# One DMA transpose in place of three pairs of PE transposes, and two moves on the DMA queue, in a block-sparse attention and spatial gating kernel

## The chip, the cores and the metric

The kernel runs on one core of a Trainium2 chip. The metric is the device time of one execution in microseconds (us), taken as the median over the timed runs. The engines are named as the profile names them: PE (TensorE, its matmuls), PEld (its weight loads), ACT (ScalarE), DVE (VectorE), POOL (GpSimd) and SP (SyncE, which issues nearly all DMAs here, in order).

## The reference

The input holds 4 batches with 8 heads, 768 positions and 64 dimensions a head. Block-sparse attention is followed by a gated feed-forward layer with a product along the sequence:

```python
scores = 1/sqrt(64) * q @ k^T                      # per batch and head, 768 x 768
scores[~mask] = -1e9                               # blocks of 32: window, edges, three sampled
attn = exp(scores - max) / sum                     # softmax
x = (attn @ v), heads side by side                 # (4, 768, 512)
h = relu(x @ w_in);  u, v = h[..., :512], h[..., 512:]
v_n = (v - mean(v)) / sqrt(var(v) + 1e-6)
v_s = w_spatial @ v_n + b_spatial                  # along the 768 positions
out = (u * v_s) @ w_out
```

## The kernel before

Heads are worked on in pairs, four pairs to a batch (pairs 0 to 3 are batch 0, 4 to 7 batch 1, and so on). A position list of 768 is six tiles of 128. For each pair, k and q are loaded, cast to bf16 (POOL), transposed so that the head's dimension lies on the partitions, and multiplied on PE; ACT takes the exponential out of PSUM into `a_all`; PE multiplies that with v (`ps_av`, one extra column gives the sum); DVE divides (`normalize`: `rc`, then `xn`). The result x is transposed once more into `xt`, so that PE can use it as the stationary operand against `w_in_t` in the feed-forward part, the class `Moe`.

The order of all instructions is written out by hand. A loop over slots `s` issues for each slot: the scores and the exponential of one unit (`qk_unit` in slots 0 to 35, `qk_full` from slot 36 on); the products with v that the table `AV_AT` puts into this slot; the functions registered with `when(slot, ...)`; `STEPS[slot]` matmuls from the queue of feed-forward steps (`run_queue`); and last the functions in `late[slot]`. Each engine works its instructions off in this order.

Batch 0 is worked in query thirds. `UNITS` lists the units: 0 and 1 are the heads of pair 0 for its first two thirds, 2 to 4 are pairs 1 to 3 in the first third, 5 to 7 pairs 1 to 3 in the second, and 8 to 11 pairs 0 to 3 in the last third, which is tiles 4 and 5 of the 768 positions. A unit takes three slots for its scores. Its normalized result is a small tile (`xn3`, two tiles of 128 by 128), and `xtr_third(u)` transposes it: two PE transposes against the identity into the spare columns of the unit's own `ps_av` bank (line 302), and one DVE copy of 128 by 256 into the pair's `xt` tile (line 221). It stands in `late` of slot 3u + 7, so slots 31, 34 and 37 for units 8, 9 and 10, and in slot 41 for unit 11. From pair 4 on, a whole pair's `xn` goes through one DMA transpose instead (`xtr_dma`, line 569).

The feed-forward products of tiles 4 and 5 of batch 0 ("v4 v5 u4 u5", four steps each, one for each pair in the order 0 to 3) are dealt into the queue in slot 42; the products with the spatial weights follow them, six steps to a tile.

Three things that the change touches go through SP. The spatial weights `w_spatial` come in six pieces (`ws_load`, line 578: four alone, the last two in one load), are cast by POOL two to a tile (`ws_cast`), and are transposed two at a time into `w_spt` by `ws_tr` (line 589) in slots 23, 27 and 31. The k, q and v of pair p are loaded by `load` (line 110; pair 6 in slot 31, pair 7 in slot 38), cast (pair 6 in slot 38), and k and q transposed by `tr_dma` into `tt` (line 444; pair 5 in slot 31, pair 6 in slot 40); `split` then copies `tt` into `kq` on DVE (line 221; pair 6 in slots 55 and 57). The load of `w_out` is registered in slot 44.

The scores lie in PSUM under the tag "sc" with two buffers of two banks each, the products with v under "av" with two buffers, and the feed-forward products in two single banks.

Of the kernel before, what the change touches and what calls it, by code (L numbers as in the profile page):

```python
# [10 lines left out]
FP32 = mybir.dt.float32  # L11
BF16 = mybir.dt.bfloat16
# [14 lines left out]
def kernel(  # L27
# [16 lines left out]
    nc = tc.nc  # L44

    B, H, S, D = q.shape
# [3 lines left out]
    NCH = S // 128  # L50
# [6 lines left out]
    NG = H // 2  # L57
# [5 lines left out]
    NT = 3  # L63
    TC = NCH // NT
# [6 lines left out]
    work = ctx.enter_context(tc.tile_pool(name="work", bufs=1))  # L71
# [379 lines left out]
    a_ref, av_ref, x_ref, xn_ref, xt_ref = {}, {}, {}, {}, {}  # L451


    UNITS = [("h", 0), ("h", 1)] + [(0, p) for p in range(1, NG)] + \
# [40 lines left out]
    def av_tile(key, n):  # L495
        ps = psum.tile([128, 512], FP32, tag="av", bufs=2, name="ps_av")
        av_ref[key] = ps[:, 0:n * VS].rearrange("p (c d) -> p c d", d=VS)
        x_ref[key] = ps[:, 512 - TW // 2:512].bitcast(BF16)

    def normalize(ps, out, n):  # L500
        rc = work.tile([128, NCH, 1], FP32, tag="rc", bufs=2)
        nc.vector.reciprocal(out=rc[:, 0:n], in_=ps[:, :, D:VA])  # L502
        nc.vector.tensor_tensor(out=out, in0=ps[:, :, 0:D],  # L503
                                in1=rc[:, 0:n].to_broadcast([128, n, D]), op=ALU.mult)

    def av_unit(u, e):
        t, p = UNITS[u]
        if e == 0:
            av_tile(u, 2 * TC)
        for i in range(8 * e, 8 * e + 8):  # L510
            g, ci = divmod(i, NCH)
            if t == "h":
                h, qc, to, n = p, g, g, 2 * TC
                pp = 0
            else:
                (h, qc), n, pp = divmod(g, TC), TC, p
                to = qc * 2 + h
            at = (h * NCH + ci) * n * 128 if t != "h" else ci * n * 128
            at += qc * 128
            nc.tensor.matmul(out=av_ref[u][:, to, 0:VA], lhsT=a_ref[u][:, at:at + 128],  # L520
                             rhs=vv[pp % NVV][:, h, ci, 0:VA],
                             start=(ci == 0), stop=(ci == NCH - 1))
        if e == 2:
            a_ref.pop(u)
            if t == "h":
                if p == 0:
                    xn_ref[0] = work.tile([128, 2 * TC, 2, D], BF16, tag="xn0", bufs=1, name="xn0")
                normalize(av_ref.pop(u), xn_ref[0][:, :, p, :], 2 * TC)
            else:
                xn_ref[u] = work.tile([128, TC, 2, D], BF16, tag="xn3", bufs=3, name="xn3")  # L530
                normalize(av_ref.pop(u), xn_ref[u].rearrange("p c h d -> p (c h) d"), 2 * TC)

    def av_full(j, qc):
# [14 lines left out]
    def xt_tile(p):  # L548
        if p not in xt_ref:
            xt_ref[p] = work.tile([128, S], BF16, tag="xt", bufs=7, name="xt")  # L550
        return xt_ref[p]

    def xtr_pe(p, xn, c0, n, ps=None):
        if ps is None:
            ps = bank()
        for c in range(n):
            tr(ps, c, pair_of(xn, c))
        dve_copy(xt_tile(p)[:, c0 * 128:(c0 + n) * 128], ps[:, 0:n * 128])

    def xtr_third(u):  # L560
# [4 lines left out]
        else:  # L565
            xtr_pe(p, xn_ref.pop(u), t * TC, TC, x_ref.pop(u))

    def xtr_dma(p):
        nc.sync.dma_start_transpose(
            out=xt_tile(p).rearrange("p (c n) -> p c n", c=NCH),  # L570
            in_=xn_ref.pop(("p", p)).rearrange("p c h d -> p (c h d)"))
# [2 lines left out]
    ws = {}  # L574

    def ws_load(i, n=1):
        t = work.tile([128, n, S], FP32, tag=f"ws_f{n}", bufs=4 if n == 1 else 1, name="ws_f")
        nc.sync.dma_start(out=t, in_=moe_w_spatial.rearrange("(p c) s -> p c s", c=NCH)[:, i:i + n])
        for k in range(n):
            ws["f", i + k] = t[:, k]  # L580
# [48 lines left out]
    class Moe:  # L629
# [9 lines left out]
            self.steps = 0  # L639

        def xt(self, g, tcc):
            return xt_ref[self.b * NG + g][:, tcc * 128:(tcc + 1) * 128]

        def v_product(self, tcc, grp):
# [121 lines left out]
    def when(slot, *fns):  # L766
        at.setdefault(slot, []).extend(fns)

    def c(f, *a, **kw):
        return lambda: f(*a, **kw)  # L770
# [14 lines left out]
    for p, sl in ((1, 12), (3, 18), (0, 21)):  # L785
        when(sl, c(tr_rest, p, 2 if p == 0 else 1))
    XT_AT = {1: 12, 3: 15, 5: 23, 11: 41}
    for u in range(1, len(UNITS)):
        late.setdefault(XT_AT.get(u, 3 * u + 7), []).append(c(xtr_third, u))
    late[15].append(c(tr_rest, 2))  # L790

    def moe_begin(b):
        moe[b] = Moe(b)
# [57 lines left out]
    def slot_of(p):  # L851
        return S0 + 12 * (p - NG)

    for p in range(NG, NP):
        g = slot_of(p)
        when({4: 13, 5: 22, 6: 31}.get(p, g - 34), c(load, p, "k"), c(load, p, "q"), c(load, p, "v"))
        when({4: 18, 5: 26, 6: 38}.get(p, g - 24),
             c(cast, p, "k", PL), c(cast, p, "q", PL), c(cast, p, "v", PL))
        when({4: 20, 5: 31}.get(p, g - (16 if p in (10, 14) else 20)), c(tr_dma, p))
        when(31 if p == 4 else g - (7 if p in (9, 13) else 5), c(split, p, 0))  # L860
        when(32 if p == 4 else g - 3, c(split, p, 1))
        if p == NP - 1:
            when(g + 20, last_x)
        else:
            when(g + (19 if p % NG == NG - 1 else 20), c(xtr_dma, p))
    for i, (ld, ca) in enumerate([(16, 19), (16, 21), (17, 23), (17, 25), (18, 27), (18, 29)]):
        if i < 5:
            when(ld, c(ws_load, i, 2 if i == 4 else 1))
        when(ca, c(ws_cast, i))
    for i, sl in enumerate((23, 27, 31)):  # L870
        when(sl, c(ws_tr, i))
    when(44, *[c(w_out_load, g) for g in range(NDH)])
    when(52, *[c(w_out_cast, g, PL) for g in range(NDH)])
# [8 lines left out]
    for s in range(NS + LAG + 2):  # L882
        if s < S0:
            qk_unit(*divmod(s, 3))
        elif s < NS:
            j, ci = divmod(s - S0, NCH)
            qk_full(j + H, ci)
        early = at.get(s, [])
        for u, e in av_at.get(s, []):
            av_unit(u, e)  # L890
        if 0 <= s - LAG - S0 and s - LAG < NS:
            j, qc = divmod(s - LAG - S0, NCH)
            av_full(j + H, qc)
        for f in early:
            f()
        run_queue(STEPS.get(s))
        for f in late.get(s, []):
            f()
        while post:
            post.pop(0)()  # L900
# [31 lines left out]
```

## Time and profile before

| | |
|---|---|
| median of 3 runs | 209.09 us (209.01 to 209.22) |
| profiled execution | 209.45 us, span 207.6 us |
| granted TensorE clock | 1.0 |
| PE busy | 202.7 us of the span |
| ACT busy | 167.0 us |
| DVE busy | 129.9 us |
| POOL busy | 75.4 us |
| DMA queue of SP | 40.78 MB, packets 76.8% of 16 engines' span |

The span runs from the first to the last instruction; the execution's own time has the launch around it. A row of a timeline gives start and length in us, the engine, the line of the kernel, the operation, what it writes and reads, and how many instructions were merged into it. PE's matmuls are pipelined, so that a busy PE may still have waited a little, and the distance between two starts says more than a duration. An SP row's length is the time of issuing; the landing of the data comes later.

### The profile page before, as it was taken

What the parts mean: (1) busy time and instruction counts of PE and PEld (TensorE: products, weight loads), DVE (VectorE), ACT (ScalarE), POOL (GpSimd) and SP (SyncE); (2) the same over time, 40 slices, a digit from 0 to 9 for tenths busy, and PEclk for the clock granted to TensorE, in tenths of its full rate; (3) what the DMA queues carried; (4) which work ended last, traced back from release to release, by engine and by line L of the source; (5) the groups of instructions that cost most, each with busy time, mean ns of one, the idle gap of its engine ahead of it and who ended that gap; (6) DMA issues with size and microseconds to landing.
All of it is one profiled execution on the core that took longest, in us unless ns stands there. A gap on an engine that the chain in (4) does not pass through costs nothing.

```text
span 207.6 us, 5255 instructions
## 1 busy us (share of the span) xinstructions
PE 202.7 (98%) x2128; PEld 127.2 (61%) x2128; DVE 129.9 (63%) x287; ACT 167.0 (80%) x222; POOL 75.4 (36%) x117
## 2 busy tenths in 40 slices
PE   8899999999999999999999999999999999999993
PEld 6689878766666666655655555655665556444441
DVE  7688697889654364648798355348685444567542
ACT  5899999999999999889999887998989883266022
POOL 6799899684680421310716402200202000003000
PEclk9999999999999999999999999999999999999999
DMA  5999999999999999999986549785101072810466
GB/s 141 345 364 347 345 406 297 234 278 303 230 356 193 264 272 171 319 318 262 299 91 182 162 88 279 179 246 125 38 3 38 0 92 51 285 72 0 50 152 255
DMA packets 65579, 42.21 MB, mean 203 GB/s; under 512 B 46740, under 2 KB 60436, under 8 KB 65556
## 3 DMA queue, kind: packets, MB, share of 16 engines
q1 hardware_dynamic: 64692, 40.78, 76.8%
q10 hardware_dynamic: 864, 1.11, 1.5%
q8 instruction: 16, 0.26, 0.5%
q14 instruction: 7, 0.06, 0.1%
HBM read 24.38 MB, written 6.29 MB: 148 GB/s over the span
## 4 chain that ended last, share of the span: by engine, by line
PE 93%; ACT 5%; issue 0%; DVE 0%; ACTq 0%
PE ps_moe L617 32%; PE ps L487 23%; PE ps_av L538 13%; PE ps_t L617 8%; PE ps L474 6%; PE ps_sc L617 5%; ACT a_all L479 5%; PE ps_av L520 4%; PE wps L182 1%; PE ps L302 1%; PE ps_av L302 1%; PE mq L309 0%; ACT osb L224 0%; PE psq L317 0%; PE ps L317 0%
## 5 line engine op out<-in xcount | busy, mean ns | idle before, releaser
L491 ACT ACTIVATE a_all<-ps 128x768 bf16<-128x768 f32 x144 | 112.8, 812 | 11.8 <-PE ps L487 5.3
L487 PE MATMUL ps<-kq 88*128 88x384 bf16 x288 | 70.4, 325 | 0.0
L538 PEld LDWEIGHTS <-a_all 128*128 128x128 bf16 x864 | 45.2, 97 | 20.0
L538 PE MATMUL ps_av<-vv,a_all 128*128 128x65 bf16 x864 | 49.8, 193 | 0.0
L487 PEld LDWEIGHTS <-kq 88*128 88x128 bf16 x288 | 27.7, 97 | 29.2 <-issue 0.3
L617 PE MATMUL ps_moe<-w_in_t,xt 128*128 128x512 bf16 x144 | 43.2, 378 | 0.0
L479 ACT ACTIVATE a_all<-ps 128x1024 bf16<-128x1024 f32 x36 | 34.1, 1026 | 2.5 <-PE ps L474 2.0
L617 PE MATMUL ps_moe<-vn,w_spt 128*128 128x512 bf16 x108 | 33.5, 378 | 0.0
L656 POOL TENSOR_SCALAR std<-mv 128x3 f32<-128x3 f32 (+1 forms) x9 | 2.9, 317 | 72.5 <-DVE mv L653 56.9
L138 POOL CAST nat<-st_k 128x768 bf16<-128x768 f32 (+2 forms) x18 | 14.6, 810 | 30.8 <-DMA st_k<-in_k_dram 29.9
L502 DVE RECIPROCAL rc<-ps_av 128x6 f32<-128x6 f32 (+1 forms) x36 | 6.7, 186 | 26.0 <-PE ps_av L538 23.2
L689 DVE SCALAR_TENSOR_TENSOR un<-ps_moe,b_col,un 128x512 bf16<-128x512 f32 x18 | 13.5, 749 | 14.8 <-PE ps_moe L617 14.8
L474 PE MATMUL ps<-kq 88*128 88x256 bf16 (+3 forms) x140 | 22.0, 279 | 0.7 <-ACT a_all L479 0.3
L617 PEld LDWEIGHTS <-xt 128*128 128x128 bf16 x192 | 15.4, 98 | 7.5 <-DVE xt L221 0.2
L503 DVE TENSOR_TENSOR xn<-ps_av,rc 128x384 bf16<-128x384 f32 (+1 forms) x36 | 18.5, 513 | 1.2
L617 PE MATMUL ps_moe<-w_out_t,gt 128*128 128x512 bf16 x60 | 17.6, 378 | 0.0
L652 DVE BATCH_NORM_STATS2 stats<-vn 128x6 f32<-128x512 bf16 x24 | 16.4, 683 | 1.3 <-ACT vn L647 0.9
L474 PEld LDWEIGHTS <-kq 88*128 88x128 bf16 (+1 forms) x140 | 12.8, 98 | 5.2 <-DVE kq L221 0.8
L138 POOL CAST nat<-st_q 128x768 bf16<-128x768 f32 (+2 forms) x21 | 14.8, 706 | 2.7 <-DMA st_q<-in_q_dram 2.2
L188 DVE TENSOR_SCALAR vn<-ps_moe 128x512 bf16<-128x512 f32 x18 | 12.3, 686 | 4.6 <-PE ps_moe L617 4.5
L617 PEld LDWEIGHTS <-w_spt 128*128 128x128 bf16 x144 | 11.7, 98 | 5.2
L221 DVE COPY kq<-tt 64x1536 bf16<-64x1536 bf16 x24 | 14.4, 598 | 0.4
(85 smaller groups left out, 208.7 us busy)
## 6 DMA issues: line engine op xcount, KB each, us to landing
st_v<-in_v_dram SPq DMA_DIRECT2D x16, 384.0 KB, 5.8
st_k<-in_k_dram SPq DMA_DIRECT2D x15, 384.0 KB, 4.7
out_dram<-osb SPq DMA_DIRECT2D x20, 256.0 KB, 2.8
st_q<-in_q_dram SPq DMA_DIRECT2D x12, 384.0 KB, 4.5
w_f<-in_moe_w_in_dram SPq DMA_DIRECT2D x6, 256.0 KB, 6.6
ws_f<-in_moe_w_spatial_dram SPq DMA_DIRECT2D x4, 384.0 KB, 7.2
w_f<-in_moe_w_out_dram SPq DMA_DIRECT2D x4, 256.0 KB, 4.2
st_q<-in_q_dram SPq DMA_DIRECT2D x6, 128.0 KB, 5.6
```

Of the source, the lines that this page charges most:

```text
L138: eng.tensor_copy(out=dst, in_=src)
L188: nc.vector.tensor_scalar(out=out, in0=in0, scalar1=s1, scalar2=s2, op0=o0, **kw)
L221: nc.vector.tensor_copy(out=o, in_=i)
L474: nc.tensor.matmul(out=ps[:, at:at + n * TW], lhsT=kq[0:kr, h, ci * 128:(ci + 1) * 128], rhs=kq[0:kr, h, qcols(t0, n)], start=True, stop=True)
L479: nc.scalar.activation(out=out, in_=ps, func=AF.Exp, scale=0.125)
L487: nc.tensor.matmul(out=ps[:, hf * 512:hf * 512 + HALF], lhsT=kq[0:KR, j % H, ci * 128:(ci + 1) * 128], rhs=kq[0:KR, j % H, S + hf * HALF:S ...
L491: nc.scalar.activation(out=a_ref["h", j][:, ci, :].rearrange("p (b c) -> p b c", b=2), in_=ps.rearrange("p (b c) -> p b c", b=2)[:, :, 0:H ...
L503: nc.vector.tensor_tensor(out=out, in0=ps[:, :, 0:D], in1=rc[:, 0:n].to_broadcast([128, n, D]), op=ALU.mult)
L538: nc.tensor.matmul(out=av_ref[j][:, qc, 0:VA], lhsT=a_ref["h", j][:, ci, qc * 128:(qc + 1) * 128], rhs=vv[p % NVV][:, h, ci, 0:VA], start= ...
L617: nc.tensor.matmul(out=ref["ps"][:, 0:w], lhsT=lhs(i), rhs=rhs(i), start=(i == 0), stop=(i == n - 1))
L652: nc.vector.bn_stats(out=stats, in_=self.vn[:, tcc, :])
L689: nc.vector.scalar_tensor_tensor(out=self.un[:, tcc, :], in0=ps, scalar=b_col[:, tcc:tcc + 1], in1=self.un[:, tcc, :], op0=ALU.add, op1=AL ...
```

## The change

Units 8, 9 and 10 (pairs 0, 1 and 2 in the last third) write their normalized results into three parts of one tile `xnl` under the tag `xn`. A new function `xtr_last`, in slot 35, issues one DMA transpose of that tile into `xtl`, a tile under the tag `xt`, six blocks of 128 columns. `Moe.xt` reads tiles 4 and 5 of pairs 0 to 2 of batch 0 from there. `xtr_third` is no longer called for units 8, 9 and 10; unit 11 keeps its place.

Pair 6's loads go from slot 31 to 36, which puts them behind the new transpose on SP. The third transpose of the spatial weights goes from slot 31 to 41, behind pair 6's `tr_dma`. Pieces 2 and 3 of `w_spatial` come in one load, as 4 and 5 did before; the buffers change from four single and one double to two of each.

```diff
@@ av_unit
-                xn_ref[u] = work.tile([128, TC, 2, D], BF16, tag="xn3", bufs=3, name="xn3")
+                if t == NT - 1 and p < NG - 1:
+                    if p == 0:
+                        xn_ref["l"] = work.tile([128, NG - 1, TC, 2, D], BF16, tag="xn", bufs=2,
+                                                name="xnl")
+                    xn_ref[u] = xn_ref["l"][:, p]
+                else:
+                    xn_ref[u] = work.tile([128, TC, 2, D], BF16, tag="xn3", bufs=3, name="xn3")
                 normalize(av_ref.pop(u), xn_ref[u].rearrange("p c h d -> p (c h) d"), 2 * TC)
+    def xtr_last():
+        xt_ref["l"] = work.tile([128, (NG - 1) * TC, 128], BF16, tag="xt", bufs=7, name="xtl")
+        nc.sync.dma_start_transpose(out=xt_ref["l"],
+                                    in_=xn_ref.pop("l").rearrange("p g c h d -> p (g c h d)"))
@@ ws_load
-        t = work.tile([128, n, S], FP32, tag=f"ws_f{n}", bufs=4 if n == 1 else 1, name="ws_f")
+        t = work.tile([128, n, S], FP32, tag=f"ws_f{n}", bufs=2, name="ws_f")
@@ Moe.xt
+            if self.b == 0 and g < NG - 1 and tcc >= NCH - TC:
+                return xt_ref["l"][:, g * TC + tcc - (NCH - TC)]
             return xt_ref[self.b * NG + g][:, tcc * 128:(tcc + 1) * 128]
@@ the tables of slots
-    for u in range(1, len(UNITS)):
+    for u in [u for u in range(1, len(UNITS)) if u not in (8, 9, 10)]:
         late.setdefault(XT_AT.get(u, 3 * u + 7), []).append(c(xtr_third, u))
+    when(35, xtr_last)
-        when({4: 13, 5: 22, 6: 31}.get(p, g - 34), c(load, p, "k"), c(load, p, "q"), c(load, p, "v"))
+        when({4: 13, 5: 22, 6: 36}.get(p, g - 34), c(load, p, "k"), c(load, p, "q"), c(load, p, "v"))
-        if i < 5:
-            when(ld, c(ws_load, i, 2 if i == 4 else 1))
+        if i not in (3, 5):
+            when(ld, c(ws_load, i, 2 if i > 1 else 1))
-    for i, sl in enumerate((23, 27, 31)):
+    for i, sl in enumerate((23, 27, 41)):
         when(sl, c(ws_tr, i))
```

## The prediction

> **What bounds the kernel now.** I read the page first, its busy shares and its chain, then the stretch of 30 to 50 us engine by engine, because the whole edit lies there, and last the queue of SyncE (SP) in the same stretch.
>
> ```profile
> span 207.6 us, 5255 instructions
> PE 202.7 (98%) x2128; PEld 127.2 (61%) x2128; DVE 129.9 (63%) x287; ACT 167.0 (80%) x222; POOL 75.4 (36%) x117
> PE 93%; ACT 5%; issue 0%; DVE 0%; ACTq 0%
> 40.00:45.00 5.00, 5.00 (x58) 3.27 (x57) 4.32 (x12) 5.00 (x7) 4.04 (x4) 1.00 0.97 226
> ```
>
> TensorE (PE) carries 93% of the chain. What PE is spared or made to wait for at 40 us should therefore reach the end undiminished, unless another engine is full at the same moment. One is: in the row of 40 to 45 us (PE, weight loads, DVE, ACT, POOL) PE and ScalarE (ACT) are both busy for 5.00 of 5.00 us. In this stage, the last slots of batch 0's query thirds and the first of batch 1, the two are nearly balanced.
>
> The profiled execution took 209.45 us around its span of 207.6; the three timed runs have the median 209.09, so the profiled one was 0.36 us slow. I work out differences in the profiled execution and take them off 209.09. About 0.2% (0.42 us) is what a measurement of this kernel can tell from no change.
>
> **Removed: three pairs of PE transposes and three copies.**
>
> ```profile
> L302 PE MATMUL ps_av<-ident,xn x20: 217/218/222, 18.5 to 45.3; 128*128 128x128 bf16 x20
> L221 DVE COPY xt<-ps_av x10: 258/286/292, 19.2 to 45.6; 128x256 bf16<-128x256 bf16 x10
> 36.68 0.28 PE L302 MATMUL ps_av<-ident,xn 128*128 128x128 bf16 x2
> 36.79 0.60 PE L474 MATMUL ps<-kq 88*128 88x256 bf16 x4
> 37.90 0.60 PE L474 MATMUL ps<-kq 88*128 88x256 bf16 x4
> 38.56 0.60 PE L474 MATMUL ps<-kq 88*128 88x256 bf16 x4
> 39.70 0.28 PE L302 MATMUL ps_av<-ident,xn 128*128 128x128 bf16 x2
> 39.81 0.60 PE L474 MATMUL ps<-kq 88*128 88x256 bf16 x4
> 40.71 0.49 PE L487 MATMUL ps<-kq 88*128 88x384 bf16 x2
> 41.53 0.49 PE L487 MATMUL ps<-kq 88*128 88x384 bf16 x2
> 42.09 0.28 PE L302 MATMUL ps_av<-ident,xn 128*128 128x128 bf16 x2
> 42.23 0.48 PE L487 MATMUL ps<-kq 88*128 88x384 bf16 x2
> 43.01 0.49 PE L487 MATMUL ps<-kq 88*128 88x384 bf16 x2
> ```
>
> A matmul's row lasts 218 ns, but matmuls overlap, so the price is the distance to the next start: 36.68 to 36.79, 39.70 to 39.81 and 42.09 to 42.23, which is 0.11 + 0.11 + 0.14 = 0.36 us. That is the most that the edit can give. The Trainium skill ("TensorE: Matmul & The Clock Gate", Part 4: PE-mode transpose) puts one transpose in a kernel's context at about 275 ns; by that figure an estimate of the gain would be 6 x 275 ns = 1.65 us. The rows of this trace speak against it: two of them take 0.11 to 0.14 us of PE's time. The three DVE copies (286 ns each) go too; PE waits for none of them here, so I count them at nothing.
>
> How much of 0.36 us survives depends on ACT. The eight L474 and L487 rows above start the scores of slots 32 to 39; each slot's exponentials follow on ACT:
>
> ```profile
> 6.09 8.32 ACT a_all L479 x9
> 36.50 1.02 ACT L479 ACTIVATE a_all<-ps 128x1024 bf16<-128x1024 f32 x1
> 37.43 1.02 ACT L479 ACTIVATE a_all<-ps 128x1024 bf16<-128x1024 f32 x1
> 38.60 1.02 ACT L479 ACTIVATE a_all<-ps 128x1024 bf16<-128x1024 f32 x1
> 39.52 1.02 ACT L479 ACTIVATE a_all<-ps 128x1024 bf16<-128x1024 f32 x1
> 40.45 1.02 ACT L479 ACTIVATE a_all<-ps 128x1024 bf16<-128x1024 f32 x1
> 41.37 0.80 ACT L491 ACTIVATE a_all<-ps 128x768 bf16<-128x768 f32 x1
> 42.06 0.82 ACT L491 ACTIVATE a_all<-ps 128x768 bf16<-128x768 f32 x1
> 42.76 0.83 ACT L491 ACTIVATE a_all<-ps 128x768 bf16<-128x768 f32 x1
> ```
>
> The first row is a stretch of the chain in which ACT alone sets the pace: nine large exponentials in 8.32 us, 0.92 us each. Between slots 31 and 36 (36.50 to 41.37) the starts stand 0.93, 1.17, 0.92, 0.93 and 0.92 us apart: one of five gaps has slack. The smaller ones stand 0.69 and 0.70 us apart. The scores of slot s go into one of two PSUM buffers (tag "sc", two buffers), so they must also wait until the exponential of slot s-2 has ended, with about 0.05 us of signalling (37.43 + 1.02 = 38.45 against the start at 38.56 shows how near that limit is).
>
> I carry the three removals through these rules. Slot 32's scores start at 36.68 instead of 36.79, but its exponential waits for ACT and gains only 0.02 (37.41). Slot 33: 37.79, exponential 38.49. Slot 34 would start at 38.45 and waits for slot 32's exponential, 37.41 + 1.02 + 0.05 = 38.48; its exponential follows at 39.41. Slot 35, with the second pair gone, starts at 39.62, exponential 40.32. Slot 36: 40.52, exponential 41.24. Slot 37 would start at 41.33 and waits for 40.32 + 1.02 + 0.05 = 41.39. Slot 38, with the third pair gone, would start at 41.95 and waits for slot 36's exponential, 41.24 + 0.80 + 0.05 = 42.09. Slot 39 then starts at 42.09 + (43.01 - 42.23) = 42.87 instead of 43.01. The gain is **0.14 us**; the other 0.22 becomes waiting of PE for ACT. The bounds are 0.14 and 0.36, and I take the lower one because the exponentials' starts leave no room for the rest.
>
> **Added: one DMA transpose, and what waits for it.**
>
> ```profile
> 38.75 3.06 SPq L444 DMA_TRANSPOSE tt<-nat  x1
> 41.86 0.58 SPq L110 DMA_DIRECT2D st_k<-in_k_dram  x1
> L569 SPq DMA_TRANSPOSE xt<-xn x11: 1211/1259/1873, 59.9 to 168.7; - x11
> DMA to landing us min/median/max: 2.7/3.0/5.4
> 40.91 0.43 DVE L503 TENSOR_TENSOR xn<-ps_av,rc 128x256 bf16<-128x256 f32 x1
> 45.57 0.10 PEld L617 LDWEIGHTS <-xt 128*128 128x128 bf16 x1
> ```
>
> In the built program the new transpose stands on SP right behind pair 5's tt transpose and ahead of pair 6's loads. The queue reaches it at 41.86, where st_k starts today. Its last input, unit 10's normalization, ends at 40.91 + 0.43 = 41.34, so nothing is waited for. It has the size of the eleven xt transposes (six blocks of 128 columns): 1.26 us of issue, and 2.7, 3.0 or 5.4 us from its start to its landing. So it lands at 44.6, 44.9 or 47.3. The first use is v4's first product in slot 42, whose weight load starts at 45.57; 0.14 earlier, that is 45.43. In the median there is 0.5 us to spare, and I count the wait at nothing. The cover is exactly that 0.5 us: PE works in order, so if the data come later, slot 43's scores and all behind stand, and each us of lateness is a us at the end.
>
> The Trainium skill speaks against this choice: "VectorE: DVE Perf Modes", The three transpose paths, sets 1309 ns for a 128x128 block by DMA against 390 ns on TensorE, and its Rules for kernel authors advise TensorE where a PSUM destination is acceptable. An estimate from that figure, six blocks one after the other, would be 7.9 us, a landing at 49.7 and a loss of some 4 us. The eleven rows above disagree, 5.4 us for six blocks at the worst.
>
> **Moved on SP and POOL.** Pair 6's three loads come behind the new transpose, 1.26 us later. The third w_spt transpose goes from its place between the loads of pairs 6 and 7 to behind pair 6's tt; these loads and tt keep their order among themselves.
>
> ```profile
> 43.88 2.84 SPq L589 DMA_TRANSPOSE w_spt<-ws_b  x1
> 46.59 1.16 POOL L138 CAST nat<-st_q 128x768 bf16<-128x768 f32 x1
> 48.48 4.04 SPq L444 DMA_TRANSPOSE tt<-nat  x1
> L444 SPq DMA_TRANSPOSE tt<-nat x12: 1457/2862/4037, 27.4 to 139.7; - x12
> 56.65 1.42 DVE L221 COPY kq<-tt 64x1536 bf16<-64x1536 bf16 x2
> 59.81 0.49 PE L487 MATMUL ps<-kq 88*128 88x384 bf16 x2
> 54.29 0.38 PE L617 MATMUL ps_moe<-vn,w_spt 128*128 128x512 bf16 x1
> ```
>
> Pair 6's q cast ends at 47.75 today; 1.26 us later is 49.0, and tt could then be issued 0.5 us later than at 48.48. Against that, the 2.84 us issue of w_spt is no longer in front. A tt that starts at 49.0 and is issued in 2.9 us lies within 0.5 us of today either way. Its reader is DVE's pair of copies at 56.65, and what they write is used in slot 60, at 59.81: behind the copies (1.42 us) stand 1.7 us of slack. Price nothing. The w_spt piece would be issued at about 52 and land by about 58. Its reader is the fifth of the products that begin at 54.29, that is 24 matmuls later at one or two a slot, beyond 65. Price nothing. The w_out loads behind it on SP come some 3 us later; their readers begin only when all 36 of those matmuls are done. The single load of two w_spatial pieces moves the same bytes, and POOL's casts follow in the same order. The seven xt buffers now hold one more tile of batch 0, which delays only pairs that come in after slot 80, long after its last use.
>
> Sum: -0.14 (bounds -0.36 and -0.14), + 0 for the landing (bounds 0 and 47.3 - 45.4 = 1.9), + 0 for the moves: 209.09 - 0.14 = **208.95**.
>
> **The rivals.**
> 1. *ACT has more room than I think*, and all 0.36 us arrive: 208.73. For it: PE is booked as never waiting in this stage. Against it: the gaps of 0.92. Chance 0.2. This still lies within 0.2%; with some 0.06 us more from the shifts between runs (the three timed runs lie 0.21 apart) it passes, and I give half of the 0.2 to that.
> 2. *The landing takes PE's place as the bound*, the case on the other side. For it: the transposes of 5.4 us exist, and the new one follows three other transposes on queues that are 0.97 busy (the DMA share in the row of 40 to 45 us). Against it: the median of 3.0. It decides from a landing at 45.43, that is 3.6 us after issue; past 3.6 + 0.14 the kernel is slower, past 3.6 + 0.14 + 0.42 = 4.1 us measurably. At the slowest row, 5.4 us, the time is 209.09 - 0.14 + 1.9 = 210.8; in the middle, 4.4 us, 209.75. Chance of measurably slower 0.27.
> 3. *The queue behind suffers*: pair 6's tt comes over 2 us later and the scores of slot 60 wait, some 0.5 us: 209.5. Chance 0.05.
> 4. *The skill's 275 ns* holds in effect: 1.65 us less by its figure, 207.4; by the rows, the most is 0.36. Chance 0.02.
>
> **How the numbers follow.** The forecast (about 0.14 gained, or the landing late by less than 0.5 us) keeps the rest, 0.46. Within 0.2%: 0.46 + 0.10 of rival 1 = 0.56. Slower by over 0.2%: 0.27 + 0.05 = 0.32. Faster by over 0.2%: 0.10 of rival 1 + 0.02 = 0.12. The range reaches from a little below rival 1 with such a shift, 208.6, to a landing about 1 us late, 209.9; beyond lies the rest of rival 2. The forecast's own range is 208.7 to 209.3.
>
> **What would show it.** Right: in the profile after, the pairs at 36.7, 39.7 and 42.1 are gone, the scores of slot 38 follow the exponential of slot 36 by 0.05 us, a small wait for ACT stands in the list of waits, the new transpose starts near 41.9 and lands before 45.4, and slot 42's first product starts 0.1 to 0.2 us earlier than 45.73. Wrong: PE or its weight load waits at 45.4 for the DMA xtl<-xnl, or the gain of slot 39 is 0.3 and more, or the new transpose starts later than 42.5 because tt before it moved.

## The result and the profile after

The changed kernel takes 211.34 us (median of 9 runs, 209.90 to 212.17) against 209.28 us for the kernel before beside it (9 runs, 209.01 to 210.47): a ratio of 1.0089 [1.0064, 1.0113]. It is slower by some 2 us, where 208.95 was forecast, and lies above the range, which ended at 209.9. Its profiled execution took 211.95 us around a span of 210.2. Every ratio in this document leaves out executions over 1.5% above the fastest of the same kernel; there are two such, 214.58 and 215.79 us, both of the kernel with two unread transposes below.

The page of the kernel after: busy time by engine, the chain by engine, and the start of the chain by line.

```profile
PE 202.3 (96%) x2122; PEld 126.3 (60%) x2122; DVE 129.1 (61%) x284; ACT 167.2 (80%) x222; POOL 74.7 (36%) x117
PE 86%; DMA 6%; ACT 5%; DVE 1%; issue 0%; ACTq 0%
PE ps_moe L628 30%; PE ps L487 21%; PE ps_av L544 12%; PE ps_t L628 7%; PE ps L474 6%; PE ps_sc L628 4%; ACT a_all L479 4%; PE ps_av L520 3%; DMA xt<-xn 3%; DMA gt<-un 2%; DMA xtl<-xnl 2%; PE wps L182 1%; PE ps L302 1%; DVE stats L665 0%; PE ps_av L302 0%; ACT kq L224 0%
```

PE's busy time fell by the 0.4 us that six transposes can explain. What is new is in the chain: DMA has 6% of it, where it had no entry, and three transfers are named. The list of waits of the kernel after says who waits for them (total, times, longest):

```profile
PEld L628 <- DMA xt<-xn: 2.0, 1, 2.0
PEld L628 <- DMA gt<-un: 1.8, 3, 0.7
PEld L628 <- DMA xtl<-xnl: 0.9, 1, 0.9
```

Of these the kernel before has only the middle one, and smaller:

```profile
PEld L617 <- DMA gt<-un: 1.2, 3, 0.5
```

The transfer `xtl` is the added one. The transfer `xt` is pair 7's, which the edit does not touch and which is due 50 us after it. PE's timeline after shows where each lands on it:

```profile
44.75 0.49 PE L487 MATMUL ps<-kq 88*128 88x384 bf16 x2
45.80 0.39 PE L628 MATMUL ps_moe<-w_in_t,xtl 128*128 128x512 bf16 x1 [0.56 <-DMA xtl<-xnl]
...
92.04 0.38 PE L628 MATMUL ps_moe<-w_in_t,xt 128*128 128x512 bf16 x1
94.14 0.60 PE L628 MATMUL ps_moe<-w_in_t,xt 128*128 128x512 bf16 x2 [1.72 <-DMA xt<-xn]
```

The first product of slot 42 starts 1.05 us after the scores ahead of it. Before, these stand 0.33 us apart:

```profile
45.40 0.49 PE L487 MATMUL ps<-kq 88*128 88x384 bf16 x2
45.73 0.38 PE L617 MATMUL ps_moe<-w_in_t,xt 128*128 128x512 bf16 x1
```

So this wait is 0.72 us. At 92.04 a product is followed by the next after 2.10 us instead of the usual 0.21: 1.89 us. That one is the fourth step of batch 1's first feed-forward product, the first to need pair 7's `xt`.

The exponentials on ACT, before:

```profile
34.62 6.86 ACT L479 ACTIVATE a_all<-ps 128x1024 bf16<-128x1024 f32 x7
41.37 2.21 ACT L491 ACTIVATE a_all<-ps 128x768 bf16<-128x768 f32 x3
```

and after:

```profile
34.10 6.72 ACT L479 ACTIVATE a_all<-ps 128x1024 bf16<-128x1024 f32 x7
40.70 3.00 ACT L491 ACTIVATE a_all<-ps 128x768 bf16<-128x768 f32 x4
```

From the first row's start to the second's it is 6.75 us before and 6.60 after: 0.15 us gained, near the 0.14 of the forecast. The same holds in every profile here: from the first of the last nine large exponentials to the first of the smaller ones it is 8.60 us in the three kernels that keep the six transposes, and 8.44 or 8.45 in the nine that do not. The remaining 0.52 of the 0.67 us by which this execution is ahead at slot 36 stood at 34.1 already, before any of the removed transposes; I do not credit it to the edit. An execution of the kernel with the transposes removed and nothing else changed (below) stands 0.35 us ahead there too.

The products at the end of the last batch, before:

```profile
198.88 1.89 PE L617 MATMUL ps_t<-w_out_t,gt 128*128 128x512 bf16 x8
200.60 1.03 PE L617 MATMUL ps_sc<-w_out_t,gt 128*128 128x512 bf16 x4
201.47 1.89 PE L617 MATMUL ps_t<-w_out_t,gt 128*128 128x512 bf16 x8
203.31 0.61 PE L617 MATMUL ps_sc<-w_out_t,gt 128*128 128x256 bf16 x4
```

and after:

```profile
200.87 1.89 PE L628 MATMUL ps_t<-w_out_t,gt 128*128 128x512 bf16 x8
202.98 1.04 PE L628 MATMUL ps_sc<-w_out_t,gt 128*128 128x512 bf16 x4 [0.22 <-DMA gt<-un]
203.85 1.89 PE L628 MATMUL ps_t<-w_out_t,gt 128*128 128x512 bf16 x8
205.91 0.61 PE L628 MATMUL ps_sc<-w_out_t,gt 128*128 128x256 bf16 x4 [0.17 <-DMA gt<-un]
```

The gaps of 1.72 and 1.84 us became 2.11 and 2.06: 0.61 us more. The ledger is -0.67 (start and gain) + 0.72 (`xtl`) + 1.89 (`xt`) + 0.61 (tail) = +2.55 us, against 2.50 between the two profiled executions (211.95 and 209.45). The largest entry is where nobody looked, so I followed SP's queue from the edit to there. After (start, length of issue):

```profile
42.39 1.56 SPq L576 DMA_TRANSPOSE xtl<-xnl  x1
...
46.70 0.47 SPq L110 DMA_DIRECT2D st_v<-in_v_dram  x1
49.76 2.22 SPq L444 DMA_TRANSPOSE tt<-nat  x1
52.02 3.46 SPq L600 DMA_TRANSPOSE w_spt<-ws_b  x1
55.53 2.00 SPq L231 DMA_DIRECT2D w_f<-in_moe_w_out_dram  x4
...
87.87 2.37 SPq L580 DMA_TRANSPOSE xt<-xn  x1
```

and before, the same two places:

```profile
52.57 0.58 SPq L231 DMA_DIRECT2D w_f<-in_moe_w_out_dram  x1
...
85.97 1.36 SPq L569 DMA_TRANSPOSE xt<-xn  x1
```

At the first load of `w_out` SP is 55.53 - 52.57 = 2.96 us late. It comes about so: pair 6's loads stand behind the new transpose, and SP then has nothing to issue from 47.17 to 49.76, because pair 6's `tt` waits for the casts on POOL:

```profile
47.97 0.82 POOL L138 CAST nat<-st_k 128x768 bf16<-128x768 f32 x1 [2.20 <-DMA st_k<-in_k_dram]
48.90 0.83 POOL L138 CAST nat<-st_q 128x768 bf16<-128x768 f32 x1
```

Before, the `w_spt` transpose (43.88 to 46.72) filled that time; now it stands behind `tt` and costs 3.46 us of its own. Between there and 87 us SP works with few pauses, and the lag stays between 2.9 and 4.2 us. At `xt` itself it is 1.90 us (87.87 against 85.97), but the issue does not set the landing. Right ahead of `xt` on SP stand the three loads of pair 11 and two stores of the output, and the last of these loads is 3.14 us late (86.27 against 83.13). From the view of DMA issues, for the stretches that hold this load or this transpose alone, median from issue to landing, first after and then before:

```profile
st_v<-in_v_dram SPq DMA_DIRECT2D x1, 384.0 KB, 5.7
xt<-xn SPq DMA_TRANSPOSE x1, 6.2
```

```profile
st_v<-in_v_dram SPq DMA_DIRECT2D x1, 384.0 KB, 5.2
xt<-xn SPq DMA_TRANSPOSE x1, 4.5
```

The load lands at 92.0 instead of 88.4, and `xt` at 94.1 instead of 90.5: both 3.6 us late, and `xt` 2.1 us behind the load each time. In all six kernels here that have these loads ahead of `xt` and whose trace has its landing, it comes 2.1 us after the last load's, with `xt` issued anywhere from 85.50 to 88.18. So the longer transfer is no loss of its own; `xt` is late because the loads ahead of it are. PE wants it at 92.0: before had 1.5 us to spare in this execution, which a lag of 3.6 us uses up, and 2 us more.

### The profile page after: what moved, and what is told of

It is laid out like the page before. It is cut to its first block, busy times and chain, and to the rows that moved or that the text cites. A ratio compares the mean times of both kernels' runs of the same rounds, so it can differ in the third digit from the quotient of the medians.

```text
span 210.2 us, 5239 instructions
## 1 busy us (share of the span) xinstructions
PE 202.3 (96%) x2122; PEld 126.3 (60%) x2122; DVE 129.1 (61%) x284; ACT 167.2 (80%) x222; POOL 74.7 (36%) x117
## 4 chain that ended last, share of the span: by engine, by line
PE 86%; DMA 6%; ACT 5%; DVE 1%; issue 0%; ACTq 0%
PE ps_moe L628 30%; PE ps L487 21%; PE ps_av L544 12%; PE ps_t L628 7%; PE ps L474 6%; PE ps_sc L628 4%; ACT a_all L479 4%; PE ps_av L520 3%; DMA xt<-xn 3%; DMA gt<-un 2%; DMA xtl<-xnl 2%; PE wps L182 1%; PE ps L302 1%; DVE stats L665 0%; PE ps_av L302 0%; ACT kq L224 0%
## 5 line engine op out<-in xcount | busy, mean ns | idle before, releaser
L628 PE MATMUL ps_moe<-w_in_t,xt 128*128 128x512 bf16 x132 | 40.0, 378 | 1.7 <-DMA xt<-xn 1.7
L138 POOL CAST nat<-st_k 128x768 bf16<-128x768 f32 (+2 forms) x18 | 14.1, 783 | 32.4 <-DMA st_k<-in_k_dram 32.0
L628 PEld LDWEIGHTS <-xt 128*128 128x128 bf16 x180 | 14.6, 98 | 9.2 <-DMA xt<-xn 2.0
L503 DVE TENSOR_TENSOR xn<-ps_av,rc 128x384 bf16<-128x384 f32 (+1 forms) x33 | 17.2, 521 | 1.1
L221 DVE COPY kq<-tt 64x1536 bf16<-64x1536 bf16 x24 | 13.8, 576 | 2.5 <-DMA tt<-nat 2.2
```

Source lines behind the costliest of these rows:

```text
L138: eng.tensor_copy(out=dst, in_=src)
L221: nc.vector.tensor_copy(out=o, in_=i)
L503: nc.vector.tensor_tensor(out=out, in0=ps[:, :, 0:D], in1=rc[:, 0:n].to_broadcast([128, n, D]), op=ALU.mult)
L628: nc.tensor.matmul(out=ref["ps"][:, 0:w], lhsT=lhs(i), rhs=rhs(i), start=(i == 0), stop=(i == n - 1))
```

## The experiments

My theory was that SP's lag, carried 40 us down a full queue, makes pair 7's `xt` late, and that the landing of `xtl` adds a little. The rivals were: the PE transposes gave nothing, or cost something by being gone; the joint load of `w_spatial` starves the weights; the new transpose's own landing is the whole loss.

**The moves alone** (before, with PE's transposes kept):

```diff
-    t = work.tile([128, n, S], FP32, tag=f"ws_f{n}", bufs=4 if n == 1 else 1, name="ws_f")
+    t = work.tile([128, n, S], FP32, tag=f"ws_f{n}", bufs=2, name="ws_f")
-    when({4: 13, 5: 22, 6: 31}.get(p, g - 34), c(load, p, "k"), ...)
+    when({4: 13, 5: 22, 6: 36}.get(p, g - 34), c(load, p, "k"), ...)
-    if i < 5: when(ld, c(ws_load, i, 2 if i == 4 else 1))
+    if i not in (3, 5): when(ld, c(ws_load, i, 2 if i > 1 else 1))
-for i, sl in enumerate((23, 27, 31)):
+for i, sl in enumerate((23, 27, 41)):
```

> The three moves without the new transpose: pair 6's loads in slot 36, the third w_spt transpose in slot 41, w_spatial pieces 2 and 3 in one load; units 8 to 10 keep their PE transposes. Theory (the loss is a lag of SP's queue that the moves make: tt of pair 5 starts 2 us late behind the joint load, tt of pair 6 waits for its casts with nothing to issue in between): the w_out loads start 2 to 3 us later than 52.57 and pair 7's xt lands near or after 92 us, so 209.4 to 210.6, with no wait at 45 us. Rival (the new transpose itself makes the lag): the w_out loads start within 1 us of before and the time is that of before, 209.1 to 209.4.

209.63 us (209.22 to 211.11): 1.0034 [1.0015, 1.0054]. Its first `w_out` load:

```profile
53.58 2.00 SPq L231 DMA_DIRECT2D w_f<-in_moe_w_out_dram  x4
```

The moves alone make SP 1.0 us late (53.58 against 52.57), not the 2 to 3 us that were expected. Pair 7's `xt` is issued at 85.99 and takes 6.0 us, so it lands at 92.0, just when it is wanted. The profiled execution (209.57 us) has no wait there; four of the other nine are 0.5 to 1.5 us longer, which a margin of nothing would explain, but the one profile does not show it.

**The third `w_spt` transpose early** (after, one line):

```diff
-for i, sl in enumerate((23, 27, 41)):
+for i, sl in enumerate((23, 27, 37)):
```

> The changed kernel with the third w_spt transpose in slot 37, between the loads of pairs 6 and 7 as before. Theory (the lag comes in good part from SP's 2.5 us of waiting at pair 6's tt): w_spt's issue fills that wait, the w_out loads start near 53.5, pair 7's xt lands before it is needed and only the 0.7 us wait for the new transpose remains: 209.3 to 210.1. Rival (the new transpose's own time and the late start of pair 5's tt make the lag): the wait at batch 1's start stays, 210.6 to 211.9.

209.47 us (209.04 to 210.70): 1.0017 [0.9999, 1.0035]. One of its waits, and its first `w_out` load:

```profile
PEld L628 <- DMA xt<-xn: 0.6, 1, 0.6
```

```profile
54.11 2.01 SPq L231 DMA_DIRECT2D w_f<-in_moe_w_out_dram  x4
```

A lag of 1.5 us instead of 3.0 leaves a wait of 0.44 us on PE instead of 1.89, and nothing waits for `xtl`, which was issued 0.35 us earlier here. So the change without the moved third makes SP about 1.5 us late, the moves without the new transpose about 1.0, and all of it together 3.0: neither part alone makes the lag. Each figure is of one execution. The kernels below have nearly the same queue up to this point and stand at 2.1 to 3.5 us with the third transpose at slot 41 and at 0.7 to 1.9 with it at slot 37, so the order is plain and the tenths are not.

**The joint load undone** (after, with `w_spatial` loaded as before):

```diff
-    t = work.tile([128, n, S], FP32, tag=f"ws_f{n}", bufs=2, name="ws_f")
+    t = work.tile([128, n, S], FP32, tag=f"ws_f{n}", bufs=4 if n == 1 else 1, name="ws_f")
-    if i not in (3, 5): when(ld, c(ws_load, i, 2 if i > 1 else 1))
+    if i < 5: when(ld, c(ws_load, i, 2 if i == 4 else 1))
```

> The changed kernel with w_spatial loaded as before (pieces 0 to 3 alone, 4 and 5 together). Theory (the joint load lands too late for POOL's third cast, and all behind it on SP starts 2 us late): pair 5's tt starts near 38.8 again, the new transpose near 41.9 and lands by about 45.2, so the wait in slot 42 falls from 0.7 to 0 to 0.4 us and the lag at the w_out loads from 3 to about 1 us: 209.3 to 210.3. Rival (the joint load costs nothing): unchanged, 210.8 to 211.9.

211.55 us (4 runs, 210.57 to 212.22): 1.0108 [1.0076, 1.0140]. The same waits as in the kernel after:

```profile
PEld L628 <- DMA xt<-xn: 1.9, 1, 1.9
PEld L628 <- DMA xtl<-xnl: 1.2, 1, 1.2
```

The expectation was missed: pair 5's `tt` starts at 41.27, not near 38.8, and the lag at the `w_out` loads is 2.9 us. No part of the loss can be seen to come from the joint load.

**The transposes removed, nothing put in their place** (before):

```diff
 def xt(self, g, tcc):
+    if self.b == 0 and g < NG - 1 and tcc >= NCH - TC:
+        tcc -= TC
-for u in range(1, len(UNITS)):
+for u in [u for u in range(1, len(UNITS)) if u not in (8, 9, 10)]:
```

> The kernel before without the three pairs of PE transposes and their copies, and with nothing in their place: the products of tiles 4 and 5 of pairs 0 to 2 read tiles 2 and 3 instead, so this part of the transposition is left out. It measures what the removal alone is worth. If ACT takes PE's place, as predicted: 0.14 us, so 0.9993 of before. If PE alone sets the pace: 0.36 us, 0.9983 of before.

209.09 us (11 runs, 208.88 to 209.57): 0.9996 [0.9986, 1.0006], that is 0.16 us less by the medians and at most 0.29. Its exponentials:

```profile
34.27 6.72 ACT L479 ACTIVATE a_all<-ps 128x1024 bf16<-128x1024 f32 x7
40.87 3.00 ACT L491 ACTIVATE a_all<-ps 128x768 bf16<-128x768 f32 x4
```

The distance is 6.60 us against 6.75 before. PE spared 0.36 us and got 0.15: the cap by ACT held, and the interval leaves out 0.36 us (0.9983). It includes no gain at all (1.0000) too; the 0.15 us rest on the exponentials. This is the most that the change could have brought.

**Pair 11's loads later** (after; they move from ahead of pair 7's `xt` on SP to behind it):

```diff
-when({4: 13, 5: 22, 6: 36}.get(p, g - 34), c(load, p, "k"), ...)
+when({4: 13, 5: 22, 6: 36, 11: 92}.get(p, g - 34), c(load, p, "k"), ...)
```

> The changed kernel with pair 11's three loads in slot 92 instead of 86, so that SP comes to pair 7's xt transpose without 1.2 MB of loads in front of it. Theory (the large loss is the wait at batch 1's first products, because SP's queue and the DMA engines run 3 us late all the way from 50 us and pair 7's xt lands at 94.1 instead of 90.5): xt is issued near 85.5 to 87, lands before 92, the wait of 1.9 us goes and 0.7 us at slot 42 stays: 209.5 to 210.1. Rival (the loss has another place and the wait only moves on): 210.8 or more.

209.62 us (209.32 to 210.31): 1.0025 [1.0015, 1.0034]. SP, and that transpose from issue to landing:

```profile
85.66 1.25 SPq L580 DMA_TRANSPOSE xt<-xn  x1
```

```profile
xt<-xn SPq DMA_TRANSPOSE x1, 2.8
```

The lag at the `w_out` loads is still 2.1 us (54.70), but this transpose no longer stands behind three loads: it is issued 2.2 us earlier than in the kernel after and lands in 2.8 us instead of 6.2, at 88.4; the wait is gone, and the ratio falls from 1.0089 to 1.0025, by the medians 1.7 us. The only edit is that three loads for a pair needed much later move past this transpose, so the theory holds for the larger part of the loss. The wait for `xtl`, which this edit cannot reach and which was expected to stay, is absent from this profile as well, so a part of the 1.7 us may be that. What is left, 0.4 to 0.5 us, is at the tail (below).

**A lag without the change** (before, with two transposes behind pair 5's `tt` that nobody reads):

```diff
+def extra():
+    for i in range(2):
+        spare = work.tile([128, NCH, 128], BF16, tag="xt", bufs=7, name="spare")
+        nc.sync.dma_start_transpose(out=spare, in_=oh)
+at[31].insert(2, extra)
```

> The kernel before with two more DMA transposes of the size of the new one behind pair 5's tt, from a constant tile into two tiles that nobody reads; nothing else is changed, and PE keeps its transposes. Theory (a lag on SP's queue is enough): two transposes delay the loads behind them by 2.5 to 3.2 us, pair 7's xt lands near 94 and batch 1's first products wait 1.5 to 2.2 us: 210.6 to 211.6. Rival (it takes the data dependence on the new transpose or the moved loads): 209.1 to 209.5.

Three executions of 210.04 to 210.44 us: 1.0047 [1.0033, 1.0061], below the 210.6 to 211.6 us that were expected. The profiled execution took 214.58 us, so its 3 us wait is more than the ratio shows. SP:

```profile
55.27 2.00 SPq L231 DMA_DIRECT2D w_f<-in_moe_w_out_dram  x4
```

and its longest new wait:

```profile
PEld L622 <- DMA xt<-xn: 3.3, 1, 3.3
```

With all PE transposes kept, the third `w_spt` in its old place and no `xtl`, a lag of 2.7 us at the `w_out` loads goes with a late `xt` of pair 7. The wait is longer than in the kernel after, at a smaller lag, so more than the lag is in it, and no run shows what; the other three executions are slower than before by 0.8 to 1.2 us, and have no profile.

**The first use of `xtl` later, too** (the edit of the pair 11 loads, and steps dealt out differently):

```diff
-STEPS = {..., 41: 2, 42: 1, 43: 3, ...}
+STEPS = {..., 41: 1, 42: 1, 43: 4, ...}
```

> As e5, and one feed-forward step of slot 41 goes to slot 42, so that the first product on the new transpose stands in slot 43 (four steps there) and is needed some 0.7 us later. Theory: both waits go, what is left is the 0.14 us that PE is spared: 208.9 to 209.4. Rival: a wait of 0.3 us or more for the new transpose stays, 209.5 to 210.1.

209.94 us (209.51 to 211.34): 1.0043 [1.0026, 1.0060], slower than with the loads alone, so the expectation was missed. No wait for `xt` or `xtl` is left; instead PE waits elsewhere, 0.4 us of it for the copy `osb` and more than before for `gt`:

```profile
PEld L628 <- DMA gt<-un: 2.0, 4, 0.7
```

Moving steps changed later slots as well; why the copy `osb` came late was not followed. One thing more can be read from this profile: SP is at least as late as in the kernel after (first `w_out` load at 56.02, `xt` of pair 7 at 88.18), yet `xt` lands at 90.9, 2.8 us after its issue, and nobody waits. The lag alone does not make `xt` late; it takes the loads ahead of it too.

**That one with the third `w_spt` at slot 37:**

```diff
-for i, sl in enumerate((23, 27, 41)):
+for i, sl in enumerate((23, 27, 37)):
```

> As e7, with the third w_spt transpose back in slot 37 between the loads of pairs 6 and 7. Theory: the lag is half as large, no wait for DMA on PE, 208.9 to 209.2, a little below before. Rival: ACT or another queue gives the 0.14 us back, 209.25 and more.

209.24 us (208.88 to 209.74): 1.0004 [0.9994, 1.0013]. Its waits for `gt` are those of before (1.2, 3, 0.5). The 208.9 to 209.2 expected, a little below before, did not come out; it is level with before.

**The tail** (the edit of the pair 11 loads, and one DVE instruction more, which writes a small constant again):

```diff
+when(60, lambda: nc.vector.memset(past, 0.0))
```

> As e5, with one small DVE memset more, in slot 60, on a constant that nobody reads any more. In the profiles so far the 319th record of DVE starts 0.40 us late in all kernels in which it is a product with the gate; in e5 it is the fourth of the last batch, and the two gt transposes behind it make PE wait 0.41 and 0.29 us near the end. Theory (the position in DVE's stream decides): one instruction more moves it off the fourth product, these waits go back to about 0.1, and the time falls by 0.4 to 0.6 us to 209.0 to 209.3. Rival (the late start belongs to the data or to the DMA queue's state at the end): unchanged, 209.5 to 209.8.

209.14 us (12 runs, 208.69 to 209.83): 0.9992 [0.9975, 1.0008]. DVE's gate products at the end, pair 11's loads late alone:

```profile
194.98 0.75 DVE L702 SCALAR_TENSOR_TENSOR un<-ps_sc,b_col,un 128x512 bf16<-128x512 f32 x1 [0.54 <-PE ps_sc L628]
196.63 0.75 DVE L702 SCALAR_TENSOR_TENSOR un<-ps_t,b_col,un 128x512 bf16<-128x512 f32 x1 [0.90 <-PE ps_t L628]
```

and with the instruction added:

```profile
194.86 0.75 DVE L702 SCALAR_TENSOR_TENSOR un<-ps_sc,b_col,un 128x512 bf16<-128x512 f32 x1 [0.54 <-PE ps_sc L628]
196.16 0.75 DVE L702 SCALAR_TENSOR_TENSOR un<-ps_t,b_col,un 128x512 bf16<-128x512 f32 x1 [0.54 <-PE ps_t L628]
```

The products follow each other by 1.65 us in the first and 1.30 in the second, after the same work of PE. One instruction more, 130 us earlier, takes the late start away, and 0.48 us of the median with it. PE waits 0.35 us for `xtl` in this profile.

**Third early and pair 11 late** (after, both one-line edits; the steps as in the change):

```diff
-when({4: 13, 5: 22, 6: 36}.get(p, g - 34), c(load, p, "k"), ...)
+when({4: 13, 5: 22, 6: 36, 11: 92}.get(p, g - 34), c(load, p, "k"), ...)
-for i, sl in enumerate((23, 27, 41)):
+for i, sl in enumerate((23, 27, 37)):
```

> The changed kernel with the third w_spt transpose in slot 37 and pair 11's loads in slot 92, and the feed-forward steps as in the change. Theory: no wait for a DMA on PE but the usual ones of the tail, and the 0.14 us that ACT leaves of the removal: 208.9 to 209.2, 0.9985 to 1.000 of before. Rival (the new transpose still lands too late in most executions): 209.4 and more.

209.17 us (12 runs, 208.78 to 210.28): 0.9997 [0.9979, 1.0015]. The waits for `xt` and `xtl` are gone and the tail is that of before. So the change can be mended to where it began; the 0.15 us that it should then be ahead is smaller than this interval, and no version measured here beats the kernel before.

## Why the prediction was wrong

**Removed: right.** 0.14 us of the 0.36 was forecast, and 0.15 (exponentials) and 0.16 (medians) were measured. PE waits for ACT where the working had put it. Rival 1, all 0.36 us, fell. So did rival 4: the Trainium skill's 275 ns for a transpose ("TensorE: Matmul & The Clock Gate", Part 4: PE-mode transpose) gives an estimate of 1.65 us for six; taking them away with nothing in their place brought 0.16 us.

**Added: the size was off.** A landing at 44.9 was forecast, against a need at 45.43. It landed at 45.75: the issue came at 42.39 instead of 41.86, and the landing 3.4 us after it instead of the 3.0 median. PE, half a us ahead in this execution, would have started that product at 45.08. This is rival 2's mechanism, 0.72 us in the profile, and it is a matter of tenths: in the kernels with this transpose it landed between 44.1 and 46.0, and PE waited between nothing and 0.97 us. PE waited in three of these profiles (after, single `w_spatial` loads, the tail's), and in just these three the two `w_spt` transposes ahead took SP 6.6 to 6.7 us instead of 5.2 to 5.3; the kernel with the transposes only removed has 6.6 as well, so this comes without the edit, and why is open. The cover of 0.5 us was less than the spread that the rows of 2.7 to 5.4 us had shown.

**Moved: the failed step.** "The w_out loads behind it on SP come some 3 us later; their readers begin only when all 36 of those matmuls are done" is right, down to the size (2.96 us). The price of nothing drawn from it is wrong, since I followed the lag to the next reader and stopped there. Everything behind on SP comes later too, and SP hardly pauses for the next 35 us (between 52 and 88 us its longest pause after is 0.52, at 68.69): the loads of pair 11 come 3.1 to 4.0 us late, and with them the landing of pair 7's `xt` behind them, by 3.6 us, whose margin of 1.5 us no row of mine had asked for. That is 1.89 us, the greater part of the loss. Even the 1.5 us are one execution's: with the transposes only removed, `xt` landed at 91.6 with next to nothing to spare. Rival 3 had the queue but sought its victim in pair 6's `tt`, which was not late enough for anyone. The Trainium skill ("Perfetto Trace Analysis", What "DMA-bound" means) names an issuing engine's sequencer that is solid with DMA work as a limit of its own; SP's rows from 52 to 88 us fit this, with PE waiting for what was issued late, even though PE was 98% busy before. They do not single it out: the DMA engines' own share is 0.99 to 1.27 in the stretches from 50 to 92 us, and `xt` lands 2.1 us behind the last load whenever it is issued.

**The tail: not foreseen.** By the experiment on the tail the 0.61 us at the end come from DVE's instruction stream, not from any data that the edit delays; it was done on the kernel with pair 11's loads late, which has the same late product. The edit takes three copies out of that stream, which the prediction counted at nothing because PE does not wait for them. No row that it looked at could have given the 0.61 us.

**The range.** It ended at 209.9, from one late landing. The two waits and the tail are separate and add up: 0.72 + 1.89 + 0.61 - 0.15 = 3.07 us in the profiled execution, of which its early start hides 0.52. The median lies 2.06 us above before, and single executions between 209.9 and 212.2, so the waits vary from one to the next.

## What to carry to other kernels

An instruction that is moved on an in-order queue delays all that stands behind it, up to the first pause that is long enough to absorb the delay: walk down the queue to that pause, and ask of each transfer on the way how much margin its reader has. Judge its landing by that of the loads ahead of it, not by its own issue. Where a transfer needed soon stands behind loads needed much later, swapping the two is worth more than shaving the queue, here 1.7 us for one number in a table. And before work is moved off the busiest engine, ask what its neighbour allows: here ACT let through 0.15 us of 0.36, less than any of the waits that the DMA path then brought.

## What the runs showed of the hardware that was not expected

**A late start on DVE by position.** In the kernels with the longer tail one gate product starts 0.42 us after the semaphore record ahead of it, where 0.07 is usual (DVE idle 0.90 us ahead of it, where it is 0.54). Counting all records of DVE with its semaphore ones, it is the 320th each time (the 319th of the expectation above counts from nought). Before, it is the third product of the last batch, whose delay is caught up by the next; after, in the run with single `w_spatial` loads and in the two with pair 11's loads late and the third at slot 41, it is the fourth, and the transpose behind it is late. In the other seven kernels the 320th record is a wait for a semaphore. One more instruction ahead moved it away. What happens at that position, no run shows.

**The clock after a long wait.** PE's longest wait here, 3.2 us in the profiled execution of the kernel with two unread transposes, was followed by a lower granted clock. A stretch of it (busy time by engine, granted clock, DMA share, GB/s):

```profile
95.40:98.80 3.40, 3.40 (x21) 1.80 (x20) 1.57 (x3) 1.00 (x2) 0.00 (x0) 0.50 1.10 364
```

For 3.4 us the clock was half, and 1.00 on both sides of it, so that in this execution the time around the wait cost more than the wait's own length. After the wait of 1.9 us in the kernel after, the clock between 94 and 96 us was 1.00. The Trainium skill ("TensorE: Matmul & The Clock Gate", Why this matters for your kernels) warns of pauses over about 3 us; both waits agree with it. It is one execution, and no run here varies the length of the wait alone.

**The same transpose, 2.7 to 6.2 us.** Pair 7's six blocks took 2.7 to 2.8 us to land in the five kernels with pair 11's loads behind them, and 4.5 to 6.2 in the six kernels with the loads ahead, at equal size. In these six they landed 2.1 us after the last load had.
